# Attention of a routed-expert kernel rewritten: tiled products in fp32, gates moved to the expert steps, and part of the first loads on ScalarE's DMA queue

## The chip, the cores and the metric

One core of one Trainium2 chip. The time is that of one execution on the device, in microseconds (us), median of several runs; beside it stands one execution that the hardware profiler recorded. Engines are named as the profile names them: PE (TensorE), PEld (its weight loads), DVE (VectorE), ACT (ScalarE), POOL (GpSimd), SP (SyncE); the DMA queue that an engine issues on is called by the engine's name.

## The reference, cut to what matters

Linear attention over 8 batches of 8 heads (576 tokens, head width 64, 128 features), then a top-1 routed layer of 8 experts over all 4608 tokens (512 wide, 1024 hidden).

```python
def phi(x):
    proj = np.einsum('bhsd,md->bhsm', x, omega)
    sq = np.sum(x * x, axis=-1, keepdims=True) / 2.0
    h = proj - sq
    h = h - np.max(h, axis=-1, keepdims=True)
    return np.exp(h) / np.sqrt(m)
q_p, k_p = (phi(q_s), phi(k_s))
kv = np.einsum('bhsm,bhsd->bhmd', k_p, v)
z = np.sum(k_p, axis=2)
num = np.einsum('bhsm,bhmd->bhsd', q_p, kv)
den = np.einsum('bhsm,bhm->bhs', q_p, z)[..., None] + 1e-06
# num / den is x of the routed layer
logits = xn @ en.T / tau                 # both of norm one
expert_idx = np.argmax(logits, axis=1)
gate_w = probs[np.arange(N), expert_idx] # softmax of logits
h = np.maximum(x[mask] @ w1[e], 0.0)
out[mask] = gate_w[mask, None] * (h @ w2[e])
```

## The kernel before, in words

The program is one straight line with two parts. Products are made on PE and read from its 8 accumulator banks by DVE and ACT.

**Attention** is a loop over `i` (L601), 43 steps over 36 tiles of 128 tokens with all 8 heads. A step works on k and v of tile `i` and on q of tile `iq = i - 6`; the first 6 steps have k alone, the last 7 q alone. Each step has two halves of 4 heads.

- `halves` (L303) splits a loaded tile of k or q into a rounded part and the rest, on POOL; `feats` (L313) projects them on omega, which is laid out as two blocks on 128 rows: 3 products of 256 columns for each two heads (high by high, high by low, low by high), 6 for a half of k and 6 for one of q, into a bank of the rotating tag `pj`. DVE takes the maximum of each row and head (L324), ACT makes 4 exponentials (L327).
- `kvmm` (L330) adds keys by values to `kva`, one product for each head, 65 columns wide (the last is the sum of keys), in fp32; an fp32 product is two instructions on PE. `qtr` (L377) transposes the features of q (L381), ACT copies one half out and DVE the other (L385, L387). PE's order interleaves these transposes with `kvmm`.
- `num` (L391) multiplies q's features by the sums of keys and values, with 8 more columns that hold the routing logits: 4 products of 73 columns for a half, in fp32 (L405), into one of two buffers of the tag `nu`; where a tile spans two batches, the products go to 64 output rows each. DVE divides (L408 to L414) and ACT sums the squares of the row (L420).
- `kvfin`, `kvfin1`, `kvfin2` (L351 to L375) turn the sums of a batch and multiply them by the normed expert embeddings (L361, L371).
- Every third tile `route` and `route1` choose the expert and the place of each token (L422, L452), and `gates` (L436) makes the softmax weight: a root in 12 small DVE operations (L114), an exponential on ACT (L444), a sum and an inverse. The weight goes into column 512 of the row of 514, POOL copies it there (L450) and scatters three tiles of rows to `xs` in HBM (L471).

k, v and q are loaded on SP (L285, L289, L300), two steps ahead. From step 27 on, the weights of the first expert are loaded and split (`first_weights`, L493), and from step 38 on, two pieces of the first two expert tiles run in each step (`first_steps`, L509); the rest of these pieces stands behind the loop, as work for PE while DVE builds the table of expert steps (L659 to L739). A piece is mostly 3 products of 512 columns.

**Expert steps** `t` from 2 to 37 (L861): 24 products for the first matrix and 24 for the second, each of 512 columns (L251), with the hidden layer turned by a DMA transpose of two 16-bit planes (L806 to L816) and put together again by DVE and ACT (L823 to L848). `scaled` (L257) multiplies the result by column 512 of the row, `store` scatters it. Each step's weights are split by DVE and POOL (L216, L217).

In both parts the order on PE and POOL is written out by hand; in the expert steps on all engines; in the attention the order on DVE and ACT is the scheduler's.

## Time and profile before

| | |
|---|---|
| three runs | 753.89 us median, 752.79 to 762.47 |
| the profiled execution | 756.55 us, of it 754.9 us from first to last instruction |
| TensorE clock granted over the span | 0.987 |
| busy: PE, PEld, DVE, ACT, POOL | 722.3, 628.6, 549.5, 381.8, 416.7 us |
| steps with k alone | 0 to 33.0 us |
| 30 steps with k and q | 33.0 to 264.5 us |
| steps with q alone, first expert pieces between | 264.5 to 311.4 us |
| table, hand-over to the expert steps | 311.4 to 335.0 us |
| expert steps 2 to 37, and the end | 335.0 to 754.9 us |

The stages are read from the first and last products of each line on PE. In a row of instructions the first two numbers are the start and the time of the group in us; a bracket names how long the engine was idle before and who ended that. In a table of stretches, busy time of PE, PEld, DVE, ACT and POOL follows the length, then the granted clock, the share of the DMA engines and GB/s. A group's busy time counts overlapping instructions once; an instruction's own time is longer than the distance to the next one, since they overlap.

### The profile page before, as it was taken

The numbers are of one execution on the slowest core, as the hardware profiler recorded it, in microseconds if no ns is written. First come the engines' busy times: TensorE is split into PE (matmuls) and PEld (weight loads), VectorE is DVE, ScalarE is ACT, GpSimd is POOL, SyncE is SP. The second block draws the span as 40 slices with busy tenths as digits, with TensorE's granted clock in tenths as the row PEclk, the third lists the DMA queues.
The fourth block names the chain that finished last, engine by engine and source line by source line (L and its number), as shares of the span: only waits on it lengthen the run. The fifth ranks groups of instructions, "written<-read, shape, count | busy, mean of one in ns | idle before, by whom it ended". The sixth has DMA issues, their size and how long they took to land. (4 is left out here: it accounts for less than half of the span.)

```text
span 754.9 us, 15226 instructions
## 1 busy us (share of the span) xinstructions
PE 722.3 (96%) x4475; PEld 628.6 (83%) x4476; DVE 549.5 (73%) x1288; ACT 381.8 (51%) x974; POOL 416.7 (55%) x385
## 2 busy tenths in 40 slices
PE   6899999999998988989999999999999999999994
PEld 6899999999888978877788888888888888888883
DVE  6468888998899888836579766686676676676661
ACT  4577777776786765425224334434434334434320
POOL 5754665677648843244456546456546546545544
PEclk9899999999999999999999999999999999999998
DMA  6543344454584421179587877977877887887730
GB/s 200 154 142 87 114 154 142 127 169 144 160 273 123 160 70 58 57 245 289 149 224 221 233 189 210 233 189 213 228 188 209 224 199 211 220 210 202 199 106 38
DMA packets 142353, 131.38 MB, mean 174 GB/s; under 512 B 106745, under 2 KB 106873, under 8 KB 142275
## 3 DMA queue, kind: packets, MB, share of 16 engines
q1 hardware_dynamic: 135954, 110.15, 53.2%
q0 software_dynamic: 6320, 20.23, 7.0%
q8 instruction: 43, 0.70, 0.4%
q14 instruction: 36, 0.29, 0.1%
HBM read 83.65 MB, written 21.80 MB: 140 GB/s over the span
## 5 line engine op out<-in xcount | busy, mean ns | idle before, releaser
L217 POOL TENSOR_TENSOR w1l<-raww,w1h 128x1024 f32 x34 | 89.0, 2616 | 158.0 <-DVE w1h L216 158.0
L251 PE MATMUL po<-w2h,hl 128*128 (+1 forms) x288 | 114.3, 397 | 0.2 <-DVE hl L847 0.2
L251 PE MATMUL po<-w2h,hh 128*128 (+1 forms) x288 | 114.4, 397 | 0.0
L251 PE MATMUL po<-w2l,hh 128*128 (+1 forms) x288 | 114.2, 396 | 0.0
L808 ACT ACTIVATE pl<-pa 128x512 uint16<-128x512 uint16 x68 | 40.4, 596 | 141.2 <-PE pa L251 130.9
L251 PE MATMUL pa<-w1h,xh 128*128 (+1 forms) x280 | 111.4, 398 | 0.0
L251 PE MATMUL pa<-w1l,xh 128*128 (+1 forms) x280 | 111.0, 396 | 0.0
L251 PE MATMUL pa<-w1h,xl 128*128 (+1 forms) x280 | 111.0, 396 | 0.0
L327 ACT ACTIVATE ftk<-pjk,nmk 128x128 f32<-128x128 f32 x288 | 82.8, 376 | 52.9 <-DVE nmk L324 27.9
L809 DVE COPY pl<-pa 128x512 uint16<-128x512 uint16 x68 | 46.8, 690 | 68.4 <-ACT pl L808 68.3
L327 ACT ACTIVATE ftq<-pjq,nmq 128x128 f32<-128x128 f32 x288 | 84.5, 396 | 13.0 <-DVE nmq L324 7.6
L827 DVE COPY wd<-t 128x1024 uint16<-128x1024 uint16 x68 | 86.0, 1269 | 0.4 <-DMA t<-pl 0.4
L217 POOL TENSOR_TENSOR w2l<-raww,w2h 128x1024 f32 x34 | 82.2, 2418 | 6.7 <-DVE w2h L216 5.3
L341 PE MATMUL kva<-vt,ftk 128*128 128x65 f32 x576 | 85.4, 260 | 0.0
L341 PEld LDWEIGHTS kva<-vt,ftk 128*128 128x128 f32 x576 | 82.4, 197 | 0.0
L381 PE MATMUL tr<-ident,ftq 128*128 128x128 f32 x288 | 75.0, 281 | 1.9 <-ACT qp L385 1.7
L405 PE MATMUL pn<-kvs,qp 128*128 128x73 f32 (+1 forms) x640 | 71.7, 264 | 3.1 <-DVE xr L414 3.1
L843 ACT ACTIVATE hh<-wd 128x1024 fp32r<-128x1024 f32 x34 | 36.1, 1061 | 72.0 <-DVE wd L827 72.0
L405 PEld LDWEIGHTS pn<-kvs,qp 128*128 128x128 f32 (+1 forms) x640 | 67.7, 182 | 5.0 <-DVE xr L414 2.3
L319 PE MATMUL pjk<-w1l,w1h 128*128 128x256 f32 x288 | 63.2, 312 | 5.5 <-DVE w1h L309 5.5
L251 PEld LDWEIGHTS po<-w2h,hl 128*128 128x128 f32 x288 | 54.2, 188 | 13.8 <-DVE hl L847 0.7
L251 PEld LDWEIGHTS po<-w2h,hh 128*128 128x128 f32 x288 | 54.3, 188 | 13.3 <-POOL w2l L217 0.3
(237 smaller groups left out, 1610.9 us busy)
## 6 DMA issues: line engine op xcount, KB each, us to landing
raww<-w1q SPq DMA_DIRECT2D x38, 512.0 KB
raww<-w2q SPq DMA_DIRECT2D x38, 512.0 KB
vt<-v SPq DMA_DIRECT2D x36, 260.0 KB
kt<-kT SPq DMA_DIRECT2D x36, 256.0 KB
qt<-qT SPq DMA_DIRECT2D x36, 256.0 KB
xgp<-xs SPq DMA_DIRECT2D x20, 257.0 KB
xg<-xs SPq DMA_DIRECT2D x18, 257.0 KB
rf<-w1q SPq DMA_DIRECT2D x4, 512.0 KB
```

Of the source, the lines that this page charges most:

```text
L217: il = nc.gpsimd.tensor_tensor(at(l, dp), raw, at(h, dp).bitcast(F32), op=ALU.subtract)
L251: done.append(nc.tensor.matmul(dst, x[:, c * P : (c + 1) * P], ws.rearrange("p o f -> p (o f)"), start=(begin and i == 0 and k == 0), stop ...
L319: nc.tensor.matmul(pj[:, 2 * a : 2 * a + 2, :].rearrange("p a m -> p (a m)"), x[:, 2 * half + a, :], o, start=n == 0, stop=n == 2,)
L327: nc.scalar.activation(ft[:, h, :], pj[:, h, :], AF.Exp, bias=nm[:, h : h + 1])
L341: nc.tensor.matmul(acc[:, h, :], ft[:, h, :], vt[:, 4 * half + h, :], start=begin and h == 0, stop=u == 4 + 4 * b and h == 3,)
L381: nc.tensor.transpose(tr[:, h * P : (h + 1) * P], ft[:, h, :], ident)
L405: nc.tensor.matmul(pn[lo:hi, h, :], qp[:, h, lo:hi], kvs[sb, b][:, 4 * half + h, :], start=True, stop=True)
L808: nc.scalar.activation(planes[1][:, o : o + 512], halved(src)[:, :, 1], AF.Copy)
L809: nc.vector.tensor_copy(planes[0][:, o : o + 512], halved(src)[:, :, 0])
L827: nc.vector.tensor_copy(to, src)
L843: nc.scalar.activation(hh, wd[:, 0:F], AF.Relu)
```

## The change

Attention is written anew; the expert steps keep their products and get the gates.

- The projection is made in plain fp32 without halves: one product for each head, 64 rows of omega by 128 columns. Even heads lie on rows 0 to 63 and odd heads on 64 to 127, and `proj` alternates between them (a head of k on the one half of the rows, one of q on the other). The bank tags are `px` and `py`, two buffers each.
- `kvmm`, `num` and `kv_logits` put out 64 rows at a time, so that there are twice as many products of the same columns, alternately to rows 0 to 63 and 64 to 127.
- The numerators have two banks of their own, `nu[0]` and `nu[1]`, allocated once; `nu[1]` also takes one of the two q transposes, `nu[0]` the turned sums. `num` does both halves at once, `num_out` reads them at the start of the next step.
- `gates` is gone. A row has 521 columns: 512 values, 8 raw logits, the number of the token. In the expert steps ACT makes the sum of squares, for three steps together a square root and three exponentials; DVE makes the norm (`norms_of`) and the inverse of the sum (`inverted`). Square root and exponential need different tables on ACT, so that 23 table loads stand there beside those of the attention.
- DVE and ACT follow an order written by hand in the loop too: `spare`, `mid` and `ends` are places in a step where the routing and the turning of the sums go. `routed` is a list of 7 pieces over four steps.
- omega (two loads) and v of tiles 0 to 3 are issued by ACT; k of tiles 0 to 3 stands first on SP. Omega is used as loaded, times a constant.
- In the loop's last steps 20 pieces of the first two expert tiles run instead of 10, of 38.

```diff
-        om = rawp.tile([P, F], F32, name="om", tag="raw_w1")[:, 0 : 2 * M].rearrange("p (a m) -> p a m", a=2)
+        om = once.tile([P, M], F32, name="om")
         for a in range(2):
-            nc.sync.dma_start(om[a * D : (a + 1) * D, a, :], omT)
+            nc.scalar.dma_start(om[a * D : (a + 1) * D, :], omT)
+        for i in range(4):
+            load(i)
...
-            nc.sync.dma_start(vt, v1[j if u < 4 else j + 1])
+                (nc.scalar if i < 4 else nc.sync).dma_start(vt, v1[r])
...
-            for a in range(2):
-                for n, (x, o) in enumerate(((hi, omh), (hi, oml), (lo, omh))):
-                    nc.tensor.matmul(
-                        pj[:, 2 * a : 2 * a + 2, :].rearrange("p a m -> p (a m)"),
-                        x[:, 2 * half + a, :], o, start=n == 0, stop=n == 2,
-                    )
+        def proj(*which):
+            for w, i, a, tag in which:
+                st["pj" + w, i, a] = ps.tile([P, 4, M], F32, name=f"pj{w}{i}_{a}", tag=tag, bufs=2)
+            for c in range(4):
+                for w, i, a, _ in which:
+                    r = slice(a * D, (a + 1) * D)
+                    nc.tensor.matmul(st["pj" + w, i, a][:, c, :], st[w, i][r, c, :], om[r, :], start=True, stop=True)
...
-                nc.tensor.matmul(
-                    acc[:, h, :], ft[:, h, :], vt[:, 4 * half + h, :],
-                    start=begin and h == 0, stop=u == 4 + 4 * b and h == 3,
-                )
+                for c in range(0, P, 64):
+                    nc.tensor.matmul(
+                        acc[c : c + 64, h, :], ft[:, h, c : c + 64], vt[:, 2 * h + a, :],
+                        start=begin and h == 0, stop=u == 4 + 4 * b and h == 3,
+                    )
...
+            parts = [(u > 4, 0, D), (u >= 4, D, P)]
+            for a in range(2):
+                for h in range(4):
+                    for b, lo, hi in parts:
+                        nc.tensor.matmul(
+                            pn[a][lo:hi, h, :], st["qp", i, a][:, h, lo:hi], kvs[sb, int(b)][:, 4 * a + h, :],
+                            start=True, stop=True,
+                        )
...
-            gates(g)
...
+            if ks and qs:
+                pairs = [("k", i, 0, "py"), ("q", iq, 1, "py")], [("k", i, 1, "px"), ("q", iq, 0, "px")]
...
+            proj(*pairs[0])
+            proj(*pairs[1])
+            if later is not None:
+                num_out(later)
+            for p in pairs[0][: 1 if i < LAG else 2]:
+                feats(*p[:3])
...
+        def squares_of(*steps):
+            for v in steps:
+                b, j = batch(v)
+                if j == 0:
+                    n2s[b] = few("n2", f"b{b}", 3)
+                squares(xg[v], n2s[b][:, j : j + 1], p2.tile([P, DM], BF16, name=f"sq{v}", tag="sq", bufs=1))
+
+        def roots_of(b):
+            rough[b] = few("rough", f"b{b}", 3)
+            nc.scalar.activation(rough[b], n2s[b], AF.Sqrt, bias=tiny)
+
+        def exps_of(b):
+            totals[b] = few("total", f"b{b}", 3)
+            for k in range(3):
+                v = NPRE + 3 * b + k
+                gates[v] = totals[b][:, k : k + 1]
+                exps(xg[v], nrms[b][:, k : k + 1], gates[v])
...
+            if t == SHIFT - 1 or t > SHIFT and t % 3 == 0:
+                roots_of(batch(t)[0])
+            elif t == SHIFT or t > SHIFT and t % 3 == 1:
+                norms_of(batch(t)[0] if t > SHIFT else 0)
+                exps_of(batch(t)[0] if t > SHIFT else 0)
+            elif t > SHIFT:
+                inverted(totals[batch(t)[0] - 1])
```

What moves on PE, in a step of the loop with k and q. Before, one half of the step (`pjk`, `pjq`: projections of k and q; `kva`: sums of keys and values; `tr`: transposes of q's features; `pn`: numerators):

```order
L319 MATMUL pjk_1_822<-w1l,w1h 128x256 x2
L319 MATMUL pjk_1_822<-w1l 128x256
...
L319 MATMUL pjq_1_836<-w1l,w2h 128x256 x2
L319 MATMUL pjq_1_836<-w1l,w2l 128x256
...
L341 MATMUL kva_1_1_491<-vt_455,ftk_1_717 128x65
L381 MATMUL tr_1_851<-ident,ftq_1_731 128x128
...
L405 MATMUL pn_0_862<-kvs_0_425,qp_0_810 128x73 x4
```

The same place now, the whole step (`nu_70` and `nu_71` are the two banks of the numerators):

```order
L322 MATMUL pjk_0_1222<-om,kt_960 128x128
L322 MATMUL pjq_1_1223<-om,qt_966 128x128
...
L322 MATMUL pjk_1_1232<-om,kt_960 128x128
L322 MATMUL pjq_0_1233<-om,qt_966 128x128
...
L346 MATMUL kva_0_0_893<-vt12v,ftk_0_1130 64x65 x8
L346 MATMUL kva_0_1_902<-vt12v,ftk_1_1178 64x65 x8
L392 MATMUL nu_71<-ident,ftq_0_1187 128x128 x4
L392 MATMUL tr_1_1286<-ident,ftq_1_1137 128x128 x4
L411 MATMUL nu_70<-kvs_1_787,qp_0_1183 64x73 x8
L411 MATMUL nu_71<-kvs_1_787,qp_1_1174 64x73 x8
```

All projections of a step now stand first, 16 of them in alternating pairs in place of 24, then the keys by values of the tile before, then the transposes by themselves, then all numerators; one fp32 product is still two instructions.

On ACT in the expert steps, from one step's last product to the next step's. Before (`hh`: hidden layer, `pl`: planes for the transpose, `wd`: words put together, `xh`: next rows):

```order
L843 ACTIVATE hh_8423<-wd_8409 128x1024
L808 ACTIVATE pl_1_8493<-pa_0_8507 128x512
L808 ACTIVATE pl_1_8493<-xg_5461 128x512
L829 ACTIVATE wd_8537<-t_31_0_8415 128x512
L829 ACTIVATE wd_8537<-t_31_1_8417 128x512
L808 ACTIVATE pl_1_8493<-pa_1_8508 128x512
L841 ACTIVATE xh_8548<-wd_8537 128x512
```

Now, in a step that ends with a root and in one that ends with exponentials:

```order
L901 ACTIVATE hh_6559<-wd_6545 128x1024
L253 ACTIVATE sq_6588,n2b_6359<-xg_5177 128x512
L921 ACT_TABLE_LOAD
L921 ACTIVATE roughb_6628<-n2b_6359,tiny 128x3
L866 ACTIVATE pl_1_6639<-pa_0_6640 128x512
...
L901 ACTIVATE hh_6684<-wd_6670 128x1024
L253 ACTIVATE sq_6714,n2b_6713<-xg_5178 128x512
L262 ACT_TABLE_LOAD
L262 ACTIVATE ex_6728,totalb_6727<-xgp_107,nrmb_6721 128x8
L262 ACTIVATE ex_6730,totalb_6727<-xg_5176,nrmb_6721 128x8
L262 ACTIVATE ex_6732,totalb_6727<-xg_5177,nrmb_6721 128x8
L866 ACTIVATE pl_1_6809<-pa_0_6843 128x512
```

The squares stand behind `hh` in every step; in two of three steps a table load and what needs it follow, all of it ahead of the first plane of the next step.

More of the change, by code (lines that the diff above doesn't have):

```diff
@@ L36 @@
 RS = 576
-PAY = DM + 2
+PAY = DM + E + 1
 NQ = 4
@@ L374, in kvfin2, with qtr @@
-                pe[:, :, 0 : 2 * E].rearrange("p c (a e) -> p c a e", a=2),
-            )
-        def qtr(i, half):
-            ft = st["fq", i, half]
-            tr = ps.tile([P, 512], F32, name=f"tr{i}_{half}", tag="tr")
+                kvs[sb, b][:, :, D + 1 :].rearrange("p (a c) e -> p c a e", a=2),
+                st["kve", sb, b].rearrange("p c (a e) -> p c a e", a=2),
+            )
+        def qtr(i, a, own):
+            tr = nu[1] if a == 0 and not own else ps.tile([P, 512], F32, name=f"tr{i}_{a}", tag="py", bufs=2)
+            st["tr", i, a] = tr
@@ L402, in num @@
-            parts = [(0, 0, P)] if u < 4 else [(1, 0, P)] if u > 4 else [(0, 0, D), (1, D, P)]
-            for h in range(4):
-                for b, lo, hi in parts:
-                    nc.tensor.matmul(pn[lo:hi, h, :], qp[:, h, lo:hi], kvs[sb, b][:, 4 * half + h, :], start=True, stop=True)
-                next(between, None)
-            rr = small.tile([P, 4], F32, name=f"rr{i}_{half}", tag="rr", bufs=3)
-            nc.vector.tensor_scalar(rr, pn[:, :, D], EPS, None, op0=ALU.add)
-            nc.vector.reciprocal(rr, rr)
@@ L597, in emb2, with go, filled @@
             nc.vector.tensor_copy(enbd[D:P, :, 1, :], ev[D:P])
-        after = {}
-        todo, later, fill = {(1, 1): [(emb1,)], (3, 1): [(emb2,)]}, None, first_steps()
+        spare, mid, ends = {}, {}, {}
+        at = lambda d, *key: d.setdefault(key, [])
+        for i, f in ((1, emb0), (3, emb1), (4, emb2)):
+            at(ends, i).append((f,))
+        later, fill = None, first_steps()
+        def go(d, *key):
+            for f, *a in d.pop(key, ()):
+                f(*a)
+        def filled(n):
+            for _ in range(n):
+                next(fill, None)
@@ new lines, in attention_moe @@
+            filling = i > NTILE
+            proj(*pairs[0])
[4 more added lines that the diff above has]
+                feats(*p[:3])
+            if 0 <= i - 1 < NTILE:
+                sb, u = divmod(i - 1, TPS)
+                for b in range(2 if i < LAG and u == 4 else 1):
+                    for a in range(2):
+                        kvmm(i - 1, a, b or int(u > 4))
+            if i < LAG:
+                feats(*pairs[0][1][:3])
@@ new lines, in attention_moe @@
+            late = bool(spare.get((i,)))
+            go(spare, i)
+            if later is not None and later % G == G - 1 and later < NTILE - 1:
+                steps = routed(later // G)
+                for d, key in ((mid, i), (ends, i), (spare, i + 1), (mid, i + 1), (ends, i + 1), (ends, i + 2), (ends, i + 3)):
+                    key = min(key, NTILE + LAG)
+                    at(d, key).append((next, steps, None))
+            go(mid, i)
+            if not qs and iq >= 2:
+                num(iq - 2)
@@ new lines, in attention_moe @@
+            if iq >= 1:
+                for a in (1, 0) if late else (0, 1):
+                    qtr(iq - 1, a, not ks)
+                qcopy(iq - 1, 1, True)
+            if 0 <= i - 1 < NTILE and u == 4 and i >= LAG:
+                for a in range(2):
+                    kvmm(i - 1, a, 1)
+            for p in pairs[1][:1]:
+                feats(*p[:3])
+            if iq >= 1:
+                qcopy(iq - 1, 0, False)
+            for p in pairs[1][1:]:
+                feats(*p[:3])
+            if filling:
+                filled(1 if i <= NTILE + 2 else 2)
@@ new lines, in attention_moe @@
+            if qs and iq >= 2:
+                num(iq - 2)
+            go(ends, i)
+            if filling:
+                filled(1)
+            n = iq - 3 * GPICK - 6
+            if 1 <= n < 2 * NQ + 1:
+                at(ends, i + 1).append((first_split, n - 1))
+            if 0 <= n < 2 * NQ:
+                first_weights(n)
+        loop.close()
+        assert not any(d for d in (spare, mid, ends)), (spare, mid, ends)
+        num_out(NTILE - 2)
+        num(NTILE - 1)
+        num_out(NTILE - 1)
@@ L741, in attention_moe @@
             next(fill, None)
-        turned(xgp[NPRE], 0, ps.tile([P, 512], F32, name="fs_x2", tag="tr"), *pre_x[0])
+        turned(xgp[NPRE], 0, ps.tile([P, 512], F32, name="fs_x2", tag="px", bufs=2), *pre_x[0])
         for _ in fill:
```

438 lines of the change are left out of this document (215 added, 223 removed).

## Prediction

> **What bounds the kernel now.** I read the stretches between the stages first, then PE in one step of the loop, then ACT and DVE in the same step, and at last the two ends of the loop and the expert steps.
>
> ```profile
> 0.00:33.00 33.00, 24.55 (x166) 23.75 (x168) 17.56 (x47) 15.03 (x49) 20.56 (x36) 0.90 0.53 171
> 33.00:264.50 231.50, 225.27 (x2106) 220.76 (x2105) 196.18 (x646) 172.53 (x586) 148.81 (x195) 1.00 0.48 151
> 264.50:311.40 46.90, 41.69 (x342) 38.61 (x342) 38.39 (x167) 28.65 (x89) 17.35 (x32) 0.96 0.15 53
> 311.40:335.00 23.60, 21.00 (x98) 16.44 (x97) 12.88 (x83) 5.97 (x11) 9.12 (x16) 0.93 0.48 159
> 335.00:745.00 410.00, 409.50 (x1769) 329.06 (x1767) 283.70 (x346) 159.60 (x239) 219.87 (x108) 1.00 0.76 205
> ```
>
> The reader sees that from 335 us on PE has half a microsecond of idle time in 410, in 1769 products of 232 ns each, and the change leaves those products alone. So the expert steps can only stay or get longer, and a gain must come from the 335 us ahead of them. There the 30 steps with k and q take 231.5 / 30 = 7.72 us each, with PE busy for 97%, DVE for 85 and ACT for 75. PE in one such half step:
>
> ```profile
> 131.21 1.01 PE L405 MATMUL pn<-kvs,qp 128*128 128x73 f32 x8
> 132.03 0.48 PE L319 MATMUL pjk<-w1l,w1h 128*128 128x256 f32 x2
> 132.82 0.40 PE L319 MATMUL pjq<-w1l,w2h 128*128 128x256 f32 x2
> 133.54 0.33 PE L341 MATMUL kva<-vt,ftk 128*128 128x65 f32 x2
> 133.71 0.28 PE L381 MATMUL tr<-ident,ftq 128*128 128x128 f32 x1
> 134.68 0.60 PE L361 MATMUL kvt<-ident,kvc 128*128 128x128 f32 x4
> 135.12 1.01 PE L405 MATMUL pn<-kvs,qp 128*128 128x73 f32 x8
> ```
>
> Groups overlap, so the distance between starts counts: 8 numerator instructions 0.82 us (131.21 to 132.03), 12 projections 1.51 (to 133.54), 8 sums and 4 transposes 1.14 (to 134.68), 4 transposes alone 0.44 (to 135.12), that is 0.11 each. A half is 3.47, a step 6.94; the other 0.8 of the 7.72 are waits and the turning of the sums. PE's own rate is the bound here.
>
> **The change, part by part.** Products that put out 64 rows are in the trace, for a tile that spans two batches:
>
> ```profile
> 288.29 0.73 PE L405 MATMUL pn<-kvs,qp 128*64 128x73 f32 x16
> 288.96 0.50 PE L251 MATMUL fs_a<-w1h 128*128 128x512 f32 x1
> ```
>
> 16 instructions take 0.67 us where 8 whole ones took 0.82, with the change of shape at both ends. Taking 0.08 us for each change (an estimate: two of them are the difference to 16 x 0.032) leaves 0.51 us, or 0.064 for a pair, so the two halves of the rows run side by side. Per step with k and q, PE's work becomes: numerators 32 instructions, 16 pairs x 0.064 = 1.0 (before 1.64); keys by values 32, also 16 pairs, 1.0; transposes 8 x 0.11 = 0.9 (both with the sums 2.28 before); four changes of shape 0.3. Projections are 16 fp32 products, 32 instructions of 128 columns. No row shows two products on different halves of the input rows. Upper bound: each goes alone at the 0.11 of a 128-column fp32 transpose, 3.5 us, more than the 3.0 now. Lower bound: pairs as in the numerators, 16 x 0.11 = 1.8. I take 1.8, since the numerators are the nearest row that has two tiles of one array. PE's sum is 5.0 us.
>
> The Trainium skill (TensorE: Matmul & The Clock Gate, Part 3, on row and column tiling) says that products on different row groups overlap and start about 4 ns apart. No run here shows it for rows; by it the projections cost the 1.8, and without it the time would be that of the second rival.
>
> Now the other engines have to follow:
>
> ```profile
> 132.50 0.60 ACT L385 ACTIVATE qp<-tr 128x512 f32<-128x512 f32 x1 [1.01 <-PE pn L405]
> 132.99 1.14 ACT L327 ACTIVATE ftq<-pjq,nmq 128x128 f32<-128x128 f32 x4
> 133.99 0.66 ACT L420 ACTIVATE sq<-xr 128x512 bf16<-128x512 f32 x1
> 132.53 0.16 DVE L408 TENSOR_SCALAR rr<-pn 128x4 f32<-128x4 f32 x1 [0.98 <-PE pn L405]
> 132.94 0.19 DVE L410 TENSOR_TENSOR lg<-pn,rr 128x32 f32<-128x32 f32 x1
> 133.05 0.41 DVE L414 TENSOR_TENSOR xr<-pn,rr 128x256 f32<-128x256 f32 x1
> 133.38 0.51 DVE L426 TENSOR_REDUCE raw<-lg 128x24 f32<-128x192 f32 x1
> 133.80 0.68 DVE L324 TENSOR_REDUCE nmk<-pjk 128x4 f32<-128x512 f32 x1
> 134.40 0.17 DVE L428 TENSOR_REDUCE mx<-raw 128x3 f32<-128x24 f32 x1
> ```
>
> ACT: four exponentials 1.0 (132.99 to 133.99), 16 of them 4.0, one copy 0.5: 4.5 a step; the squares are gone. DVE: four maxima at 0.6 (133.80 to 134.40) 2.4, a copy of the same 512 columns 0.6, both halves of the numerators 0.4 + 2 x (0.11 + 0.33) = 1.3, a third of the routing (0.42 for the sum of logits, some ten small ones at 0.1 to 0.2) 0.7, the turned sums 0.2: 5.2 a step. So all three engines stand between 4.5 and 5.2, and the order decides. The longest ring that I find goes through the banks `px`: projections of k1 and q0 0.9 (they need the banks that the last exponentials of the step before give back), keys by values 1.0, both transposes 0.9, ACT's copy 0.5 and behind it, in ACT's fixed order, the exponentials of k1 and q0, 2.0. That is 5.3; two changes of shape (0.16), the tail of the last transpose (0.28 - 0.11 = 0.2) and four hand-overs of some 0.07 make 6.0. Numerators and the first pair of projections lie beside ACT's part, DVE's division beside PE's projections. I add 0.25 for steps in which POOL's or PE's extra work (weights of the first expert, turned sums, a tile in two batches) touches the ring. 28 steps x 6.25, and the first two, which have no numerators yet, at 4.7: 184.4 us in place of 231.5, **47.1 less**.
>
> DMA: a step loads 0.77 MB and scatters 0.26, 165 GB/s at 6.25 us, and 247 with the weights of the first expert; the second row of stretches moved 151 at a share of 0.48, so some 310 at full share. Hidden, with half a step or more to spare.
>
> The beginning:
>
> ```profile
> 0.98 1.21 SPq L557 DMA_DIRECT2D om<-omT  x2
> 2.24 0.58 SPq L285 DMA_DIRECT2D kt<-kT  x1
> 3.74 0.29 DVE L561 TENSOR_SCALAR om<-om 128x256 f32<-128x256 f32 x1 [2.13 <-DMA om<-omT]
> 5.54 0.80 PE L319 MATMUL pjk<-w1l,w1h 128*128 128x256 f32 x2 [5.54 <-DVE w1h L309]
> 21.29 0.41 PE L594 MATMUL eps__340<-ident,embq 8*128 8x8 f32 x4 [2.35 <-DVE embq L589]
> ```
>
> k0 is issued 1.26 us earlier and needs no split, so the first product comes at 4.0 in place of 5.54. Six steps with k alone are 0.9 + 1.0 + 0.16 on PE and 2.0 on ACT; two run at half clock (the first stretch's mean is 0.90) at 3.9, four at 2.4 with hand-overs; with 0.6 for the expert embeddings they end at 22.0 in place of 33.0, **11 less**. The wait of 2.35 us at 21.29 goes, since the root now lies on POOL between steps 1 and 3. ACT's six issues and its table load stand ahead of its first exponential at about 5.3, when the first maximum is not yet made. Of the 11, what moved queue is worth 1.3.
>
> The steps with q alone and the hand-over:
>
> ```profile
> 310.41 1.01 PE L405 MATMUL pn<-kvs,qp 128*128 128x73 f32 x8
> 315.89 0.16 DVE L466 CAST posi<-pos 128x3 int32<-128x3 f32 x1
> 319.75 0.43 POOL L450 COPY xr<-gt 128x1 f32<-128x1 f32 x3 [6.11 <-DVE gt L448]
> 326.05 0.35 SPq L169 DMA_DIRECT2D xgp<-xs  x1
> 328.82 0.63 PE L237 MATMUL fs_x<-ident,xgp 128*128 128x128 f32 x4 [2.05 <-DMA xgp<-xs]
> 335.01 0.39 PE L251 MATMUL pa<-w1h 128*128 128x512 f32 x1
> ```
>
> A step with q alone is 3.2 us of PE (projection 0.9, transposes 0.9, numerators 1.0, changes of shape 0.4) and the pieces, 0.7 each: 4.1, twice 4.7, three times 5.9, and 5.5 to the last numerators, 37 in place of 45.9 (264.5 to 310.41). From there the places took 5.5 us; the scatter then waited for the weight column until 319.75. Now it follows at once, 3.9 earlier, less 0.5 for both halves in one; so the rows of step 2 are turned at 18.4 - 3.4 = 15.0 after the last numerators. No piece is left to stand behind that, so step 2 starts 2 us later (transposes 0.45, copies 0.6 and 0.7, hand-overs), at 17.0 in place of 24.6. Together 54 in place of 70.5, **16.5 less**.
>
> The expert steps:
>
> ```profile
> 511.04 0.60 ACT L808 ACTIVATE pl<-pa 128x512 uint16<-128x512 uint16 x1 [4.13 <-PE pa L251]
> L327 ACT ACT_TABLE_LOAD x1 | 1.3, 1283 | 1.0 <-PEq L1012 1.0
> L420 ACT ACTIVATE sq<-xr 128x512 bf16<-128x512 f32 x36 | 23.1, 643 | 14.7 <-DVE xr L414 10.6 <-DVE mx L428 2.2 <-DVE gt L448 1.2
> L444 ACT ACTIVATE ex<-ex 128x24 f32<-128x24 f32 x12 | 2.8, 237 | 2.2 <-DVE ex L443 2.2
> PE po L251 <- DVE hl L847: 0.2, 1, 0.2
> ```
>
> ACT is idle for 4.1 us ahead of the first plane, exactly where squares (0.64, 0.2 to read the sum), a table load (1.28) and a root (0.24) or three exponentials (0.7) now stand: 2.4 or 2.9 us, after five small DVE operations of 0.15. They fit, so I cost them at nothing; without that cover they are the first rival. For the start of the steps, with weights closer behind and a clock that drops after the wait, I add 2 us: 421.9 from step 2 to the end in place of 419.9.
>
> Sum: 754.9 - 47.1 - 11 - 16.5 + 2 = 682.3. The profiled execution's span is 1.0 above the median of the runs, within their scatter; I predict **682 us**, 9.5% less.
>
> **Rivals.** First, slower than before: the moved gates land on PE's path. In three expert steps they are 3 x 0.84 + 2 x 1.28 + 0.24 + 0.7 = 6.0 us on ACT and 1.1 on DVE; all of it exposed costs 7.1 x 34 / 3 = 80 us, 762. It beats the gain from 6.4 us per three steps on. Against it stands the idle 4.13 of every step.
>
> The Trainium skill (ScalarE: Activation LUTs, What ACT_TABLE_LOAD costs) gives 2.66 us for a switch, 1.28 for the load and 1.38 for the drain; 23 switches would add an estimated 32 us to that rival, 794. No run here shows a switch; with 4.13 idle, one of 2.66 and the squares still fit.
>
> Second: row pairs run one after the other. 0.9 more in the ring of 28 steps, 0.9 in some 12 steps with k or q alone: 682 + 36 = 718. Third: the fixed order costs more, since DVE at 5.2 with its waits for numerators and transposes joins the ring; a step of 7.0 gives 28 x 0.75 = 21 more, 703. Fourth: the ring hides its hand-overs (5.7 a step) and the beginning ends at 20: 664.
>
> **How the numbers follow.** Forecast 0.72, third rival 0.12, second 0.07, fourth 0.05, first 0.04. The forecast's own range is 668 to 698 (0.4 us a step is 11, beginning and hand-over 4). The range 664 to 712 takes in the third and fourth and half of the way to the second. Slower by over 2% (above 769, which a measurement here tells from no change) is the upper part of the first, 0.02; within 2% the rest of it and the unforeseen, 0.04; faster 0.94.
>
> **What would show it.** Right: pairs of projections with 0.11 us between pairs, a step near 6.2 us with PE, DVE and ACT each busy for 75 to 88%; steps with k and q from 22 to 206 us; step 2 of the experts near 260; 232 ns for each product there and PE without waits for ACT. Wrong: 0.22 between pairs; DVE busy without gaps in the loop; PE waiting in the expert steps for planes or for `xl`; a start beyond 27.

## The result

The changed kernel takes 715.75 us (median of four runs, 714.67 to 717.12), the kernel before 753.34: a ratio of 0.951 with a 95% interval of 0.948 to 0.954. So it is faster, by 4.9%, about half of what was forecast, and 3.75 us above the upper end of the range. The profiled execution takes 715.37 us, with a span of 713.7. Now and then an execution of the same kernel is a few per cent longer, and ratios and intervals leave these out.

The stretches of the kernel after, cut where its stages meet; the columns are those of the same table before (length, busy time of PE, PEld, DVE, ACT and POOL, granted clock, DMA share, GB/s):

```profile
0.00:24.60 24.60, 17.09 (x293) 15.24 (x294) 10.45 (x31) 14.45 (x51) 4.77 (x31) 1.00 0.63 202
24.60:220.00 195.40, 181.66 (x3319) 161.60 (x3317) 158.42 (x481) 151.33 (x525) 47.91 (x98) 1.00 0.55 181
220.00:270.80 50.80, 43.07 (x536) 35.83 (x536) 33.68 (x124) 25.19 (x78) 18.32 (x42) 0.93 0.18 60
270.80:288.40 17.60, 14.78 (x76) 11.70 (x70) 10.78 (x68) 1.68 (x3) 6.88 (x12) 0.90 0.39 146
288.40:705.00 416.60, 410.10 (x1768) 328.70 (x1768) 357.80 (x431) 225.57 (x420) 223.08 (x113) 1.00 0.77 206
```

| stage | before | forecast | after | after less forecast |
|---|---|---|---|---|
| steps with k alone | 33.0 | 22.0 | 24.6 | +2.6 |
| 30 steps with k and q | 231.5 | 184.4 | 195.4 | +11.0 |
| steps with q alone, hand-over | 70.5 | 54.0 | 68.4 | +14.4 |
| expert steps 2 to the end | 419.9 | 421.9 | 425.4 | +3.5 |

The loop no longer holds PE busy for 97% (93 now), and the steps with q alone take longer than before (50.8 us for 45.9). DVE in the expert steps went from 284 us busy of 410 to 358 of 417 and ACT from 160 to 226, while PE and PEld hardly moved (409.5 to 410.1 and 329.1 to 328.7). The next rows are one loop step on PE, in the order of time, with the pairs at its start:

```profile
127.70 0.37 PE L322 MATMUL pjk<-om,kt 64*128 64x128 f32 x1
127.71 0.37 PE L322 MATMUL pjq<-om,qt 64*128 64x128 f32 x1
127.92 0.27 PE L322 MATMUL pjk<-om,kt 64*128 64x128 f32 x1
127.92 0.27 PE L322 MATMUL pjq<-om,qt 64*128 64x128 f32 x1
128.03 0.27 PE L322 MATMUL pjk<-om,kt 64*128 64x128 f32 x1
128.03 0.27 PE L322 MATMUL pjq<-om,qt 64*128 64x128 f32 x1
128.87 0.37 PE L322 MATMUL pjq<-om,qt 64*128 64x128 f32 x1
129.96 1.15 PE L346 MATMUL kva<-vt21v,ftk 128*64 128x65 f32 x32
131.04 0.66 PE L392 MATMUL nu<-ident,ftq 128*128 128x128 f32 x4
132.06 1.25 PE L411 MATMUL nu<-kvs,qp 128*64 128x73 f32 x32
133.24 0.37 PE L322 MATMUL pjk<-om,kt 64*128 64x128 f32 x1
```

A product of k and one of q, on the two halves of the rows, start within 0.01 us, and the next pair 0.11 later, as the forecast had it. Sums take 1.08 us (129.96 to 131.04), transposes 1.02, numerators 1.18, projections 2.26; the first pair after another shape takes 0.21, not 0.11, so a change of shape costs more than the 0.08 I took. Without waits the projections take 1.98, so PE needs 5.26 a step, not 5.0. But this step of 5.54 is one of the shortest; the mean over the 28 steps that the forecast put at 6.25 is 6.55.

### The profile page after: what moved, and what is told of

It reads as the page before. It is cut to its first block, busy times and chain, and to the rows that moved or that the text cites. A ratio compares the mean times of both kernels' runs of the same rounds, so it can differ in the third digit from the quotient of the medians.

```text
span 713.7 us, 17997 instructions
## 1 busy us (share of the span) xinstructions
PE 666.7 (93%) x5977; PEld 553.1 (77%) x5978; DVE 571.1 (80%) x1134; ACT 418.2 (59%) x1074; POOL 301.9 (42%) x296
## 5 line engine op out<-in xcount | busy, mean ns | idle before, releaser
L242 PE MATMUL nu<-w2h,hh 128*128 (+1 forms) x288 | 113.9, 396 | 0.7 <-POOL w2l L208 0.6
L242 PE MATMUL nu<-w2l,hh 128*128 (+1 forms) x288 | 113.6, 395 | 0.0
L242 PE MATMUL nu<-w2h,hl 128*128 (+1 forms) x288 | 113.6, 394 | 0.0
L322 PE MATMUL pjk<-om,kt 64*128 64x128 f32 x576 | 75.3, 292 | 7.3 <-DVE om L575 5.9
L322 PE MATMUL pjq<-om,qt 64*128 64x128 f32 x576 | 75.5, 284 | 4.6 <-ACT ftq L331 3.9
L322 PEld LDWEIGHTS pjk<-om,kt 64*128 64x128 f32 x576 | 65.7, 195 | 10.2 <-DVE om L575 5.6
L322 PEld LDWEIGHTS pjq<-om,qt 64*128 64x128 f32 x576 | 63.4, 187 | 8.3 <-ACT ftq L331 5.6
L242 PEld LDWEIGHTS nu<-w2h,hh 128*128 128x128 f32 x288 | 54.3, 188 | 14.0 <-POOL w2l L208 1.4
L242 PEld LDWEIGHTS nu<-w2h,hl 128*128 128x128 f32 x288 | 54.2, 188 | 12.7
L242 PEld LDWEIGHTS nu<-w2l,hh 128*128 128x128 f32 x288 | 54.2, 188 | 12.6
```

What stands on the lines that cost most here:

```text
L242: done.append(nc.tensor.matmul(dst, x[:, c * P : (c + 1) * P], ws.rearrange("p o f -> p (o f)"), start=(begin and i == 0 and k == 0), stop ...
L322: nc.tensor.matmul(st["pj" + w, i, a][:, c, :], st[w, i][r, c, :], om[r, :], start=True, stop=True)
```

## The experiments

All times are medians; the base is the changed kernel at 715.75 us, unless another is named.

**The second pair begins with q** (e1_alternate). The gap between 128.03 and 128.87 looked like a loss on PE where two products use the same half.

```diff
-                for w, i, a, _ in which:
+                for w, i, a, _ in which[::-1] if flip else which:
...
-            proj(*pairs[1])
+            proj(*pairs[1], flip=True)
```

> Base is the changed kernel (715.7 us). The second group of projections in a step starts with q instead of k, so that the halves of the rows go on alternating (now two products on the same half follow each other there, and 8 pairs at 0.105 us turn into 1.1 and 1.16 us with 0.25 lost at the junction). Theory A, PE's own products set the step (5.54 us in a plain step: projections 2.25, sums 1.08, transposes 1.02, numerators 1.18): projections 2.0 a step, 0.2 to 0.25 us less in each of 30 steps, 708 to 711 us. Theory B, the fixed order on DVE and ACT sets the step: projections 2.0 as well, but PE waits by as much more, 715 to 716 us.

Measured: 715.15 us (713.62 to 716.53), steps of 6.55 us. Theory B has the time, but the projections did not get shorter either: 2.25 us in the median, as before, since the second group still waits for its bank. That wait for `ftq` comes to 3.0 us in eight steps here and 2.7 in seven in the changed kernel; PE's waits between 36 and 206 us here:

```profile
PE nu L411 <- DVE qp L400: 4.1, 8, 0.7
PE pjk L322 <- ACT ftq L331: 3.0, 8, 0.8
```

So a gap that is closed on PE opens again at the bank, and PE's own rate alone does not hold a step. Read again, the rows of the changed kernel give a chain that closes over two steps:

```profile
127.68 1.14 ACT L331 ACTIVATE ftq<-pjq,nmq 128x128 f32<-128x128 f32 x4
133.35 0.16 DVE L424 TENSOR_SCALAR rr<-nu 128x4 f32<-128x4 f32 x1 [0.20 <-PE nu L411]
134.69 0.68 DVE L328 TENSOR_REDUCE nmk<-pjk 128x4 f32<-128x512 f32 x1
135.41 1.14 ACT L331 ACTIVATE ftk<-pjk,nmk 128x128 f32<-128x128 f32 x4 [0.52 <-DVE nmk L328]
139.93 1.16 ACT L331 ACTIVATE ftq<-pjq,nmq 128x128 f32<-128x128 f32 x4
```

ACT gives the bank back at 128.82; PE projects q into it at 128.87 and goes on with sums, transposes and numerators; DVE divides at 133.35 and takes the maximum behind that; ACT's four groups and its copies end at 141.09. That is 4.5 on PE, 2.1 on DVE and 5.7 on ACT, 12.27 us for two steps, or 6.13 each, with a tile of two batches and its extra copy among them.

**Both copies of the transposed features on ACT** (e8_copies) lengthen ACT's part of that chain.

```diff
-                qcopy(iq - 1, 0, False)
+                qcopy(iq - 1, 0, ks)
```

> Both copies of the transposed features on ACT instead of one on ACT and one on DVE, in the 30 steps with k and q. Theory A (a ring of two steps sets the pace: ACT's four groups of exponentials and its copy, 4.66 us from the first to the last without a gap, then PE's second projections, sums, transposes and numerators, 4.5, DVE's division and maximum, 2.2): ACT's part gets 0.5 us longer, 0.25 to 0.5 a step, 722 to 731 us. Theory B (DVE's order sets the pace, and its copy, which waits for PE, is what holds it): 0.3 to 0.6 a step less, 698 to 707 us.

Measured: 750.16 us, ratio 0.994 (0.990 to 0.997); a step of 7.69. Theory A has the sign, though not the size: the second copy stands on ACT behind the exponentials of k, the numerators' second half waits for it (1.3 to 1.7 us in the steps that I read), and the chain now closes in one step.

**The transposes in one order** (e9_natural) take away the wait of 0.34 to 0.9 us that the numerators have where the order is reversed.

```diff
-                for a in (1, 0) if late else (0, 1):
+                for a in (0, 1):
```

> The changed kernel with the transposes of q always in one order, the half that goes to the second bank of the numerators first. In steps with routing or turned sums on PE the order is reversed, and there the second half of the numerators waits for DVE's copy: 1.52 or 2.08 us instead of 1.18, in two steps of three. Theory A (that wait is on the path, and the bank is free in time): 0.3 us less in 20 steps, 708 to 711 us. Theory B (PE then waits as long for DVE to have read the bank): 714 to 718 us.

Measured: 717.13 us (715.18 to 720.91), numerators 1.35 instead of 1.49 on average over the 28 steps, but a step of 6.59. Theory B: the wait only goes elsewhere.

**Row halves one after the other** (e2_serial) and **whole products for sums and numerators** (e4_whole) take back one kind of tiling each.

```diff
-            for c in range(4):
-                for w, i, a, _ in which:
+            for w, i, a, _ in which:
+                for c in range(4):
```

> The four heads of one tile are projected one after the other before those of the second tile, so that successive products use the same half of the input rows; the same products otherwise. Theory A (halves of the rows run side by side, and PE sets the step): 0.105 us for each instruction instead of each pair, projections 3.5 instead of 2.25 a step, 30 steps by 1.2 and some of it in the steps with k or q alone: 745 to 760 us, so that most of the change's gain hangs on the alternation. Theory B (DVE and ACT set the step): under 10 us more.

```diff
-                for c in range(0, P, 64):
...
-                        acc[c : c + 64, h, :], ft[:, h, c : c + 64], vt[:, 2 * h + a, :],
+                        acc[:, h, :], ft[:, h, :], vt[:, 2 * h + a, :],
...
-            parts = [(u > 4, 0, D), (u >= 4, D, P)]
+            parts = [(0, 0, D), (1, D, P)] if u == 4 else [(u > 4, 0, P)]
```

> Sums of keys by values and numerators put out 128 rows at once again, half as many products. Theory A: one whole product costs 0.10 us an instruction as before the change (8 in 0.82), where a pair of halves costs 0.058, so sums 1.6 instead of 1.08 and numerators 1.65 instead of 1.18, 1.0 us a step: 738 to 748 us. Theory B (a whole product costs the same as a pair, the columns set it): 714 to 717 us.

Measured: 733.13 us (ratio 0.973, 0.966 to 0.980) and 748.32 (744.54 to 765.97, 746.5 without the three longest; ratio 0.992, 0.987 to 0.997). The first lies between its two theories, the second is theory A. In the first the projections take 3.09 instead of 2.26 and a step 7.13; sums and numerators of the second kernel in one of its steps:

```profile
112.48 2.00 PE L346 MATMUL kva<-vt16v,ftk 128*128 128x65 f32 x16
114.32 0.60 PE L392 MATMUL nu<-ident,ftq 128*128 128x128 f32 x4
115.20 1.90 PE L411 MATMUL nu<-kvs,qp 128*128 128x73 f32 x16
117.03 0.37 PE L322 MATMUL pjk<-om,kt 64*128 64x128 f32 x1
```

16 whole instructions take 1.84 us, 0.115 each, where 16 pairs of halves take 1.08 or 1.18. So the row halves are worth 17 us of the whole and the column halves 31 to 33, together more than the 38 that the change gained (no run took both back). PE's waits between 36 and 206 us, 9.1 us in the changed kernel, fall to 4.7 and 2.6 in these two: PE sets the pace again, which is why these show and e1 did not.

**The first loads.** Omega alone back to SP (e3_om_sp), and all of it on SP in the old order (e14_one_queue).

```diff
-            nc.scalar.dma_start(om[a * D : (a + 1) * D, :], omT)
+            nc.sync.dma_start(om[a * D : (a + 1) * D, :], omT)
```

> Omega's two loads go back to SP's queue, first in line; v of the first four tiles stays on ACT's. In the changed kernel omega was ready at 5.65 us, after 1 MB of k had been issued beside it; before, alone in front, at 3.74. Theory A (omega shares the DMA engines with k and so comes late): first product near 4.1 instead of 5.9, and the whole 1.5 us shorter, 713 to 715 us. Theory B (the wait for k is as long): first product after 5.3, 715 to 717 us.

```diff
-                (nc.scalar if i < 4 else nc.sync).dma_start(vt, v1[r])
+                nc.sync.dma_start(vt, v1[r])
```

> Everything of the first loads on SP's queue again, omega first, then k and v of a tile in turn, as before the change; the rest as changed. With v on ACT's queue omega came at 5.65 us behind k, and at 6.28 in front of it; before, at 3.74. Theory A (two queues share the DMA engines from the start, so nothing that is first in line comes first): omega near 3.8, k0 near 5.1, first product at 5.1 to 5.3, 0.7 us less at the start, and later tiles as before: 714 to 716 us. Theory B (omega's late arrival has another cause): first product after 5.8 us, no gain.

Measured: 716.17 us (714.0 to 718.39) and 716.52 (714.27 to 716.64): no difference in the whole beyond the spread of the runs. The starts do differ: with omega alone on SP the first product came at 8.64 us, not near 4.1, so theory B holds there; with one queue omega came at 3.88 and the first product at 5.18, as theory A has it. The changed kernel, omega alone on SP, and one queue, in this order:

```profile
0.98 1.94 SPq L297 DMA_DIRECT2D kt<-kT  x4
0.98 1.20 ACTq L572 DMA_DIRECT2D om<-omT  x2
5.65 0.23 DVE L575 TENSOR_SCALAR om<-om 128x128 f32<-128x128 f32 x1 [4.46 <-DMA om<-omT]
5.93 3.79 PE L322 MATMUL pjk<-om,kt 64*128 64x128 f32 x32 [5.93 <-DVE om L575]
```

```profile
6.28 0.23 DVE L575 TENSOR_SCALAR om<-om 128x128 f32<-128x128 f32 x1 [5.10 <-DMA om<-omT]
8.64 1.65 PE L322 MATMUL pjk<-om,kt 64*128 64x128 f32 x12 [8.64 <-DMA kt<-kT]
```

```profile
3.88 0.23 DVE L575 TENSOR_SCALAR om<-om 128x128 f32<-128x128 f32 x1 [2.69 <-DMA om<-omT]
5.18 2.08 PE L322 MATMUL pjk<-om,kt 64*128 64x128 f32 x16 [5.18 <-DMA kt<-kT]
```

With two queues at work from the start, two loads of 32 KB that stand first in theirs land 1.8 to 2.4 us later than with one, and k too, in the second kernel. The Trainium skill (DMA: Bandwidth & Descriptors, Rules for kernel authors) says that queues of different engines run on the same 16 DMA engines and interleave, so that spreading loads over them brings no bandwidth; these runs agree.

**Without the gates** (e7_nogate), to see what they cost in the expert steps.

```diff
-                squares(xg[v], n2s[b][:, j : j + 1], p2.tile([P, DM], BF16, name=f"sq{v}", tag="sq", bufs=1))
+                gates[v] = one32
...
-            nc.scalar.activation(rough[b], n2s[b], AF.Sqrt, bias=tiny)
+            pass
...
-                inverted(totals[batch(t)[0] - 1])
+                pass
```

> Leaves out the softmax weights in the expert steps from 2 on: no squares, roots, exponentials and table loads there, rows are scaled by one. Theory A: they stand in idle time of ACT, and the 5.4 us by which the expert steps got longer is the late rows of steps 2 and 3: 713 to 716 us. Theory B: the gates are that loss (three steps with 0.4 to 0.65 us more, 1.0 at the end, and part of the start): 709 to 712 us.

Measured: 701.68 us (699.11 to 703.91), ratio 0.931 (0.925 to 0.937): 14 us less, more than either theory allowed. The cause shows in the number of products that PE starts in the same 160 us, first the changed kernel, then this one:

```profile
480.00:640.00 160.00, 159.88 (x688) 128.60 (x687) 148.35 (x175) 92.40 (x175) 86.83 (x43) 1.00 0.81 213
```

```profile
480.00:640.00 160.00, 160.00 (x708) 132.52 (x707) 124.45 (x148) 67.04 (x103) 88.51 (x44) 1.00 0.85 219
```

PE is idle for 0.12 us in the first and not at all in the second, the granted clock is 1.00 in both, and still 708 products stand against 688. From start to start a product takes 226 or 227 ns here, and 228 to 241 ns in the changed kernel, in a pattern that repeats about every seven products. Leaving the gates out had also moved every tile in SBUF. Four runs asked whether the start of a tile or the gates' work does this (the last has a second such tile at the head of the expert steps' tiles):

```diff
+    spare8 = const.tile([P, 8], F32, name="spare8")
     ident = const.tile([P, P], F32, name="ident")
```

> The changed kernel with 32 unused bytes a partition ahead of everything, so that the weights of the expert steps and their other operands start at a multiple of 64 bytes (before: multiples of 64 plus 32); nothing else. In the run without gates, where the same bytes had moved by another constant tile, a product of the expert steps took 227 ns throughout instead of 232. Theory A, the start address sets this and the gates cost nothing: 227 ns here too with all gates in, 12 us less, 702 to 705 us. Theory B, the gates' work on ACT and DVE slows the products: 232 ns, 714 to 717 us.

> The kernel before with the same 32 unused bytes: the moving operand (weights) then starts at a multiple of 64, the stationary one (rows of tokens) at 32 past one; before it was the other way round and a product took 234 ns. If the moving operand's start decides: 227 ns, 14 us less, 739 to 742 us. If the stationary one's does or both must be aligned: 230 to 234 ns, 750 to 756 us. Theory B of the run above: 753 to 756 us.

> The run without gates (rows scaled by one in the expert steps, no squares, roots, exponentials and table loads there) with 32 unused bytes more, so that both operands of the expert products start at 32 past a multiple of 64 again, as in the changed kernel. There a product took 227 ns, with gates and either start 232 to 233. Theory A (the gates' work slows each product by some 6 ns): 227 ns, 700 to 704 us. Theory C (only both at a multiple of 64 and no gates together are fast): 232 ns, 712 to 716 us.

> The kernel before, which has no gates in the expert steps, with unused bytes at two places, so that both operands start at a multiple of 64. Theory A (gates): it has none and still takes 234 ns, so something else must slow it; unchanged, 751 to 757 us. Theory C (both starts and no gates): 227 ns, 739 to 743 us.

Measured: 714.92 us for the changed kernel with everything moved by 32 bytes, 753.95 and 758.9 (748.49 to 765.48) for the kernel before moved at one place or two, 703.49 without gates and moved. Neither the start modulo 64 nor the gates' work explains all of these. What fits them all is how far apart the two operands start (the addresses are those that the built programs give to weights and turned rows):

| kernel | distance modulo 256 bytes | ns a product (median) |
|---|---|---|
| before; before moved at one place | 96 | 234 |
| after; after moved; before moved at two places | 128 | 232 |
| without gates; the same moved | 0 | 227 |

**The distance alone** (e15_gap, and e16_before_gap with 104 columns in the kernel before):

```diff
     p2 = ctx.enter_context(tc.tile_pool(name="p2", bufs=2))
+    gap = p2.tile([P, 32], F32, name="gap", bufs=1)
```

> The changed kernel with 128 unused bytes a partition at the head of the expert steps' tiles, nothing else. Theory D: what slows a product is how far apart its two operands start. Over the runs, the distance from the weights to the turned rows, modulo 256 bytes, was 96 in the kernel before and with its weights shifted (234.3 ns a product), 128 in the changed kernel, with everything shifted, and in the kernel before with both starts moved (232.4 to 233.7), 0 in the two runs without gates (226.7). Here it becomes 0: 226.7 ns, 12 us less, 702 to 705 us with all gates in. Theory A (gates slow the products): 232 to 234 ns, 714 to 717 us. If the period is 512 (the runs without gates had 0, this one has 256), also 714 to 717 us.

> The kernel before with 416 unused bytes at the same place: the distance becomes 154112 bytes, the very one of the runs without gates. Theory D: 226.7 ns a product, 13 us less, 739 to 743 us, so that the pace of the products was no part of the change. Otherwise 234 ns, 752 to 756 us.

Measured: the kernel before with the gap takes 739.33 us (738.8 to 751.38), ratio 0.972 (0.963 to 0.982), 227 ns a product; its row over the same 160 us:

```profile
480.00:640.00 160.00, 160.00 (x708) 132.53 (x707) 124.45 (x149) 68.60 (x105) 90.19 (x45) 1.00 0.82 216
```

Theory D. The gap moves all tiles of the expert steps alike against the weights; that the product's own operand matters, and not another tile that moved with it, is likely but not isolated. The changed kernel with the gap has 227 ns too, but takes 712.55 us (712.39 to 713.29; the kernel before was spread from 753 to 764 beside it, so times are compared, not ratios), 3.2 less instead of 12. From the first product of the second matrix to the end it is 406.2 us, and 407.4 without the gap: only 1.2 of the 3.2 lie in the expert steps, and the rest may be spread. The faster products do not add up to more of them in the same 160 us (689, and 688 without the gap):

```profile
480.00:640.00 160.00, 158.59 (x689) 128.09 (x688) 147.12 (x176) 91.57 (x169) 88.40 (x45) 1.00 0.80 210
```

Now PE waits; from 300 us on:

```profile
PE pa L242 <- DVE xl L905: 4.1, 11, 1.2
PE nu L242 <- POOL w2l L208: 0.9, 1, 0.9
```

**The gates without DVE's part** (e18_nonorm, on top of the gap; a larger gap keeps the distance).

```diff
-            nc.vector.reciprocal(nrms[b], rough[b])
...
+            nrms[b] = rough[b]
...
-                inverted(totals[batch(t)[0] - 1])
+                pass
```

> The 128-byte run with part of the gates left out: ACT's squares, roots, exponentials and table loads stay, DVE's seven small operations for three steps (norm and inverse of the sum) go, the root is the scale and the sum the factor. With 227 ns a product PE waits for DVE's part of the hidden units (0.3 to 0.5 us, twice in three steps), and the expert steps take 406 us where those without any gates took 395.5. Theory A (DVE is the second bound, busy 91%, and its 1.2 us for three steps are what PE waits for): 702 to 705 us. Theory B (ACT's squares and table loads delay the planes): 710 to 713 us.

Measured: 701.02 us (699.55 to 706.01), below theory A's range and far from theory B: with ACT's squares, roots, exponentials and table loads (24 in the trace, not 23) all there, the time is that of the runs without any gates. Seven operations of 0.17 us for each three steps are some 14 us of DVE's time in all. They cost 11.5 us of the whole (712.55 - 701.02), 11.1 of it from the first product of the second matrix to the end (406.2 and 395.2). The waits for DVE in the view above come to 4.1 only, since it counts them from the end of a product that lasts 0.39 us; from start to start, the products there lose 10.8 us beyond 227 ns each in the run with the gap and 1.5 without DVE's part, 6.9 of the 10.8 ahead of products that need `xl`. The edit also takes away ACT's own waits for the norm, 3.2 us in eleven, which are not told apart here. The copies of 16-bit planes show where DVE loses more than these operations last; over the same 160 us, with the gap, and then without DVE's part:

```profile
L886 DVE COPY wd<-t 128x1024 uint16<-128x1024 uint16 x30 | 51.0, 1699 | 0.0
L868 DVE COPY pl<-xg 128x512 uint16<-128x512 uint16 x9 | 17.2, 1908 | 1.1 <-DMA xg<-xs 1.1
```

```profile
L886 DVE COPY wd<-t 128x1024 uint16<-128x1024 uint16 x29 | 37.0, 1276 | 0.0
L868 DVE COPY pl<-xg 128x512 uint16<-128x512 uint16 x8 | 7.2, 901 | 0.0
```

The same copies take a third longer, or twice as long, with the small operations there. In both runs almost half of the 128x1024 copies begin during one of POOL's subtractions (33 and 32 of 68), and each of these ends 0.61 to 0.64 us behind it; a copy that meets none takes 0.73 to 0.78. What differs is how much of the subtraction is left when the copy begins: 2.1 us in the median with the small operations, 1.6 without. So they seem to shift the copies against POOL's work; no run shifted the copies alone. One such meeting, in the changed kernel:

```profile
472.70 0.77 DVE L885 COPY wd<-t 128x1024 uint16<-128x1024 uint16 x1
473.66 2.42 POOL L208 TENSOR_TENSOR w2l<-raww,w2h 128x1024 f32 x1
473.95 2.77 DVE L885 COPY wd<-t 128x1024 uint16<-128x1024 uint16 x1
```

The copy takes 0.77 us alone; the second begins 0.29 after POOL's subtraction and ends 0.64 after it, as if it had stood still until then. The Trainium skill (SBUF — State Buffer, SBUF: two separate sides) describes a port pair that one of VectorE, in its two-port modes, and GpSimd holds for a whole instruction while the other blocks; this row agrees.

**The hand-over.** Turning pieces moved to the middle of a step (e6_turns), and the numbers of the last two tiles copied ahead of POOL's scatters (e5_ids).

```diff
-                filled(1 if i > NTILE + 2 else 0)
+                filled(1 if i > NTILE + 2 or i == NTILE + 1 else 0)
...
-            if filling:
+            if filling and i not in (NTILE + 1, NTILE + 5):
                 filled(1)
```

> In the last steps of the loop, the two pieces that turn rows or hidden units and ended a step (behind which DVE's subtraction stood ahead of the division of the numerators) run in the middle of a step; one of 20 pieces moves behind the loop's last but one step. Theory A (the 14 us that steps with q alone took over the forecast are PE's waits for DVE behind those pieces, 2.3 and 2.8 us, and the halved clock after them): 51 us from the end of the steps with k to the last numerators become 43 to 46, 707 to 711 us. Theory B (the pieces are PE's own work): 714 to 716 us.

```diff
+            if i == NTILE + LAG:
+                for t in range(NTILE - 2, NTILE):
+                    row(t)
             go(ends, i)
```

> The changed kernel with POOL's copies of the token numbers of the last two tiles ahead of the three scatters of the group before, instead of behind them. DVE waited 2.1 us for them after the last numerators (273.19 us), and table and rows of the second expert step follow. Theory A (on the path to that step): 1.5 to 2.1 us less, 713 to 715 us. Theory B (the rows of the next step, which wait for the scatters, set the start of the steps): under 0.5 us.

Measured: 711.66 us (709.61 to 714.58) and 714.38 (712.98 to 715.45). In the first, the steps with q alone, taken up to the product behind their last numerators, took 47.9 us instead of 51.0, but the two waits it was meant to remove are still there:

```profile
PE nu L377 <- DVE xr L431: 2.9, 1, 2.9
PE nu L456 <- DVE xr L431: 2.7, 1, 2.7
```

Moving the pieces on PE left DVE's two subtractions ahead of the division in DVE's own order, so the edit did not do what it was for. The same steps took 49.3 to 52.9 us in the profiles of the kernels without it, and 49.3 in the next run, which has it too, so most of the 4 us may be chance. The second lies in theory A's range, but the stretch that it was to shorten, from the last numerators to the first product of the second matrix, came to 34.6 us, and to 32.8 to 36.2 in the kernels without it: no gain shows there, as theory B has it, and the 1.4 us of the whole are within the spread.

**All three together** (e17_best: gap, turns, numbers):

> The changed kernel with the three things that helped: 128 bytes between the operands of the expert products (3.2 us less), turning pieces in the middle of a step (4.1 less), token numbers ahead of the scatters (1.3 less). Theory A (three places, the gains add): 706 to 708 us, 6% less than the kernel before. Theory B (the last two shorten the same wait): 708 to 711 us.

Measured: 712.58 us (710.42 to 713.06), ratio 0.945 (0.942 to 0.948), what the gap alone gives, and above both ranges. The other two bring nothing that adds; e6 alone had come out lower than all three together.

No run gave DVE and ACT back to the scheduler's order or put the gates back into the attention, so what these two parts of the change are worth is not shown.

## Why the prediction was wrong, by its steps

**The loop: sign and pairs right, the ring that sets the step wrong.** Pairs on two row halves at 0.11, 16 pairs in 1.08 and 1.18 for sums and numerators instead of 1.0: shown by the rows, and by e2 and e4. Failed: "I add 0.25 for steps in which POOL's or PE's extra work touches the ring", on a ring of 6.0 that "goes through the banks px". The shortest steps do take 5.54 to 6.02, but the mean is 6.55. The chain that closes over PE, DVE and ACT passes through the division, which I had put "beside PE's projections"; what routing and the turned sums add to any of the three engines then lands on it. That is the reading that the rows and the sign of e8 support; no run took the routing or the turned sums out. The 28 steps took 183.5 us in place of 175, 8.5 of the 11; the other 2.5 are the first two steps, 11.9 in place of 9.4, in which PE waits 2.1 us for ACT's exponentials. A step of 6.55 lies between the forecast and the third rival (7.0), whose reason, DVE in the ring, fits the chain. The Trainium skill (TensorE: Matmul & The Clock Gate, Part 3) has products of different row groups start about 4 ns apart; here they start some 7 ns apart.

**The steps with q alone failed most.** "37 in place of 45.9" became 50.8, more than before. The forecast summed PE's products and pieces and left out who waits for whom.

```profile
235.15 0.65 PE L377 MATMUL nu<-enbd,kvts 128*64 128x16 f32 x16 [2.34 <-DVE xr L431]
263.07 0.18 PE L456 MATMUL nu<-sel,tri 128*128 128x32 bf16 x1 [2.80 <-DVE xr L431]
263.25 2.02 PE L411 MATMUL nu<-kvs,qp 128*64 128x73 f32 x32
```

The turned sums and the routing write into the numerators' own two banks, so they wait until DVE has divided, and DVE had the subtractions of the expert pieces ahead of that. PE's waits in this stage come to about 7.7 us; the numerators behind the second take 1.94 us to the next group instead of 1.18, and the granted clock of 0.93 over 50.8 us makes some 3 us more. The rest of the 13.8 stays open. The cause of the waits is read from the rows; that their removal gains the time was not shown, since e6 left them in place. The hand-over itself, 17.0, measured 17.6.

**The beginning** failed at "the first product comes at 4.0": it came at 5.93, when omega was there. With one queue it came at 5.18, so the second queue cost 0.75 where I had counted 1.3 as its gain; and even then PE waited for k, which I had there by 4.0. The steps behind the first product took 18.7 us, 18.0 in the forecast. So the gain of 8.4 owes nothing to the queue.

**The expert steps.** "I cost them at nothing" held, in part by luck: from the first product of the second matrix to the end it is 407.4 us, and 407.0 before (a 512-column product took 232 ns in the one and 234 in the other; the forecast's 232 was a mean of all of PE's products).

```profile
347.89 0.39 PE L251 MATMUL po<-w2h,hh 128*128 128x512 f32 x1
```

```profile
288.37 0.50 PE L242 MATMUL pa<-w1h 128*128 128x512 f32 x1 [0.69 <-ACT w1h L229]
293.86 0.41 PE L228 MATMUL pt<-ident,xg 128*128 128x128 f32 x2 [2.23 <-DMA xg<-xs]
306.34 0.39 PE L242 MATMUL nu<-w2h,hh 128*128 128x512 f32 x1
```

The start is what got longer: 306.34 - 288.37 = 18.0 us in place of 347.89 - 335.01 = 12.9, with 2.23 of waiting for rows; I had added 2. But the cover was named wrongly. I looked at ACT, and ACT's part does cost nothing (e18). DVE's part costs 11 us as soon as the products are not slowed for another reason, and then the sign that the forecast named, PE waiting for `xl`, is there: the first rival, with DVE in place of ACT, hidden behind the distance of two operands. The two limits lie 1.2 us apart (406.2 with fast products and DVE's part, 407.4 with slow ones), which no step of the forecast foresaw. The Trainium skill (ScalarE: Activation LUTs, What ACT_TABLE_LOAD costs) gives 2.66 us a switch with the drain; here the load alone shows:

```profile
478.24 0.19 ACT L253 ACTIVATION_READ_ACCUMULATOR sq<-xgp 128x1 f32 x1
478.45 1.28 ACT L262 ACT_TABLE_LOAD   x1
480.00 0.30 ACT L262 ACTIVATE ex<-xg,nrmb 128x8 f32<-128x8 f32 x1 [0.27 <-DVE nrmb L930]
```

It starts 0.02 us behind the instruction ahead, and the exponential 0.27 after its end, when DVE was done.

## What to carry to other kernels

When several engines are each busy for 80 to 95% of a step, follow one chain across the engines and over step ends until it closes, in each engine's own order, before adding "extras": here the division stood on it and had been taken for hidden. An experiment that leaves work out also moves tiles, so its gain belongs to the work only when a second run with the work in, and the tiles moved, has shown it. Small operations on an engine that another can hold up may cost what they shift, and not only what they last: between 310 and 690 us DVE is busy for 343 us with the seven operations (e15) and for 299 without them (e18), though they last some 16 themselves.

## What the runs showed of the hardware

- A 512-column product took 227 ns when its two operands started a multiple of 256 bytes apart, 232 at 128 and 234 at 96 (modulo 256), in ten kernels; in the kernel before that is 11.7 us of the expert steps from the first product of the second matrix on (407.0 and 395.3, e16). Other distances were not tried, the cause is open, and neighbouring tiles moved along.
- 16 pairs of halves of 64 output rows took 1.08 us at 65 columns and 1.18 at 73, 16 whole products 1.84: worth 31 to 33 us here.
- A 128x1024 16-bit copy on DVE of 0.73 to 0.78 us takes until 0.61 to 0.64 us behind POOL's subtraction when it begins during one (2.77 in the row shown).
- Two queues loading from the start delayed omega, first in its own, by 1.8 to 2.4 us against one queue.
